# Attention and experts on one core: product with v in one step, a hand-made order, q cast on GpSimd

## The chip, the cores and the metric

One core of a Trainium2 chip runs the whole program. Its engines are TensorE (PE; PEld is its weight load), VectorE (DVE), ScalarE (ACT), GpSimd (POOL) and SyncE (SP, which issues transfers here). The metric is the time of one execution on the device in microseconds, as the median of several executions.

## The reference, cut to what matters

Attention with 8 batches, 8 heads, 576 positions and 64 values per head, then a mixture of 8 experts in which each token goes to one.

```
scores = q @ k.T / 8 + cum[i] - cum[j]        # cum = cumsum(log(clip(f)))
attn   = softmax(scores, causal)              # per batch and head, 576 x 576
x      = attn @ v                             # rows of all heads: 4608 x 512
e      = argmax(x @ w_gate); g = softmax(x @ w_gate)[e]
out    = g * (relu(x @ w1[e]) @ w2[e])        # w1: 512 x 1024, w2: 1024 x 512
```

All inputs and the output are float32.

## The kernel before, in words

**Pairs and steps.** Attention runs over 32 pairs of heads (n = 4 b + p: batch b, pair p). `attention_all` has one outer loop over n, from 0 to 33, and in it seven steps, i = 0 to 6 (lines 540 to 574). Step i of pair n issues one group of scores of pair n (`s_steps`: the causal tiles of both heads, then the last 64 queries of both heads jointly), one group of transposes of the weights of pair n - 1 (`t_steps`), and, at i = 1 and i = 4, one part of the product with v of pair n - 2 (`av`). At the other steps one task is taken off a list, `todo`, that finishes a batch (`fin_tasks`): the gate's product, rows of x divided by their sums and written to DRAM, and the routing stages of `route_stages`.

**Scores.** Scores are nearly exact in float32 though they are made of two fp32r products (`smm`, lines 263 to 273): the first has 128 rows, q's high part on rows 0 to 63 and q's low part on rows 64 to 127 (tile `qk1`), against k's high part twice; the second has 68 rows, q's high part again with four rows of sums (tile `q2`), against k's low part and four rows (tile `k2`). DVE adds the mask, writes to `sc` and keeps the smallest value (`s_red`, line 276); ACT takes the exponential and its sum (`s_exp`, line 283).

**Splitting q and k.** `split(n + 1)` at step 0 of pair n (lines 210 to 242): ACT casts q and k of `raw` to `qk1` (lines 228 and 229), a transfer on ACT's queue copies q's high part to `q2` (line 238), GpSimd subtracts for the low parts (`lo`, line 217), and SP loads the rows of sums from the DRAM tables cq and ck (lines 231 and 232). For n = 0 and 1 the rows of sums come straight from `cw` (`c_rows`, lines 244 to 255), partly on GpSimd's queue. `raw` has two buffers, and pair 2 a third; `load_pair(n + 3)` stands at step 5 of pair n, `load_v(n + 2)` at step 3.

**Transposes and product.** Transposes go to PSUM, and ACT (tiles 3 and 2) or DVE (the rest) copies them to `aT`. `av` (lines 382 to 404) has two parts: queries 320 to 575 with five blocks of keys, the last of 64 rows (`vb_t`), and queries 0 to 319 with three. Both heads' outputs share one PSUM bank, `ps_v`, and ACT copies each part to `xT`.

**Order.** The program is traced in this order, and a scheduler with a simulated timeline reorders what each engine gets, by what it takes to be ready; `tc.issue_after` holds TensorE's steps in their order. Each engine's queue then runs in order, and an instruction waits for semaphores at the head of its queue. SP's queue carries the loads and the writes of x alike.

**Hand-over to the experts.** Tokens are ranked within their expert. Expert 0's first 384 slots are filled from all batches but the last (`LATE = 1`, line 784): after batch 6's table, `early_tasks` work out the indices, gather rows from x in DRAM, and transpose them. Then `Moe.run` does the up products (`up`, line 890, 12 matmuls each) of those slots, gathers the other two blocks, and goes on with `down` (line 912). In `onehot_hi` the five products for the table (line 734) run on GpSimd, but on DVE where `last` is set, which is for b >= B - 2 (line 1103). Expert 0's w1 is split by DVE (high part, line 796) and GpSimd (low part, line 797).

Of the kernel before, what the change touches and what calls it, by code (L numbers as in the profile page):

```python
# [19 lines left out]
P = 128  # L20
# [10 lines left out]
class Ctx:  # L31
    pass

# [33 lines left out]
def setup_consts(c, tc):  # L67
    c.ident = c.const.tile([P, P], F32, name="ident")
    make_identity(tc.nc, c.ident)
    c.identr = c.const.tile([P, P], F32R, name="identr")  # L70
    tc.nc.vector.tensor_copy(c.identr, c.ident)


def attention_all(c, tc, qkT, va, vb, f, wgd, x_dram, batch_done, more_consts, extra):
# [13 lines left out]
    SO = {3: 0, 2: 512, 0: 896, 1: 1024}  # L88
    HW = 1280
    AS = 448  # L90

    with ExitStack() as st:
# [22 lines left out]
        def load_pair(n):  # L115

            pool, tag = (c.xap, "xa") if n == 2 else (c.wp, "R")
            raw = pool.tile([P, QW + 2 * S], F32, name="raw", tag=tag)
            b, p = divmod(n, NPAIR)
            for c0, c1 in ((0, QW), (QW, QW + 2 * S)) if n == 0 else ((0, QW + 2 * S),):  # L120
                for p0 in (0, HD):
                    last = nc.sync.dma_start(raw[p0 : p0 + HD, c0:c1], qkT[b, p, :, c0:c1])
            raws[n] = raw
            return last
# [6 lines left out]
        cq = dr.tile([2, NPR, 2, 640], F32, name="cq")  # L131
# [3 lines left out]
        nc.sync.dma_start(fr, f)  # L135
        load_pair(0)
        V.memset(ones, 1.0)
# [5 lines left out]
        nc.scalar.activation(warm, fr[0:1, 0:1], AF.Exp)  # L143
# [15 lines left out]
        Q2s, K2s = [], []  # L159
        for i in range(NQ):  # L160
            q2 = ap_.tile([68, QW], F32R, name=f"q2_{i}")
            k2 = ap_.tile([68, 2, S], F32R, name=f"k2_{i}")
# [4 lines left out]
            Q2s.append(q2)  # L167
            K2s.append(k2)
# [15 lines left out]
        setup_consts(c, tc)  # L184

# [4 lines left out]
        def late_consts():  # L190
            V.memset(wg, 0.0)
            for j in range(2):
                nc.sync.dma_start(
# [6 lines left out]
        vts, xTs, ssums, jsums = {}, {}, {}, {}  # L200

        def load_v(n):
            b, p = divmod(n, NPAIR)
            va_t = io.tile([P, 4, 2, HD], F32, name="va_t")
            vb_t = io.tile([64, 2, HD], F32, name="vb_t")
            nc.sync.dma_start(va_t, va[b, p])
            nc.sync.dma_start(vb_t, vb[b, p])
            vts[n] = (va_t, vb_t)

        def split(n):  # L210
            q2, k2 = Q2s[n % NQ], K2s[n % NQ]
            raw = raws.pop(n)
            qk1 = c.qp.tile([P, QW + 2 * S], F32R, name="qk1", tag="Q")
            q2c = q2[64:66].bitcast(F32).rearrange("r (j s) -> r j s", j=2)
            k2c = k2[66:68].bitcast(F32)
            k2l = k2[0:64].rearrange("p j s -> p (j s)")
            lo = lambda eng, o, p0, c0, c1: eng.tensor_tensor(  # L217
                o, raw[p0 : p0 + 64, c0:c1], qk1[p0 : p0 + 64, c0:c1].bitcast(F32),
                ALU.subtract,
            )  # L220
            if n == 0:
                nc.scalar.copy(qk1[:, 0:QW], raw[:, 0:QW])
                nc.scalar.copy(qk1[:, QW:], raw[:, QW:])  # L223
                nc.scalar.copy(q2[0:64], raw[0:64, 0:QW])
                lo(V, qk1[64:128, 0:QW], 64, 0, QW)
                lo(V, k2l, 0, QW, QW + 2 * S)
            else:
                nc.scalar.copy(qk1[:, 0:QW], raw[:, 0:QW])  # L228
                nc.scalar.copy(qk1[:, QW:], raw[:, QW:])
                if n > 1:  # L230
                    nc.sync.dma_start(q2c, cq[:, n].rearrange("j r s -> r j s"))
                    nc.sync.dma_start(
                        k2c.rearrange("r j s -> r (j s)"), ck[n].rearrange("r j s -> r (j s)")
                    )
                if n == 1:
                    V.tensor_copy(q2[0:64], raw[0:64, 0:QW])
                else:
                    nc.scalar.dma_start(q2[0:64].bitcast(F32), qk1[0:64, 0:QW].bitcast(F32))
                eng = V if n == 1 else nc.gpsimd
                lo(eng, qk1[64:128, 0:QW], 64, 0, QW)  # L240
                lo(eng, k2l, 0, QW, QW + 2 * S)
            ops[n] = (qk1, qk1[:, QW:].rearrange("p (j s) -> p j s", j=2), q2, k2)

        def c_rows(n):

            q2c = Q2s[n][64:66].bitcast(F32).rearrange("r (j s) -> r j s", j=2)
            k2c = K2s[n][66:68].bitcast(F32)

            eng = nc.sync if n == 0 else nc.gpsimd
            eng.dma_start(k2c[:, 0, :], cwf[n : n + 1, :, 0:S])  # L250
            eng.dma_start(q2c[:, 0], cwf[n : n + 1])
            hb = NPR + n
            nc.gpsimd.dma_start(k2c[:, 1, 0:512], cwf[hb : hb + 1, :, 0:512])
            nc.gpsimd.dma_start(k2c[:, 1, 512:S], cwf[hb : hb + 1, :, S:640])
            return eng.dma_start(q2c[:, 1], cwf[hb : hb + 1])
# [31 lines left out]
        def s_tiles(n, items):  # L287
# [9 lines left out]
            for j, t in items:  # L297
# [3 lines left out]
                s_exp(n, d, w, 5 * j + t,  # L301
                      ssums[b][:, t, 2 * p + j : 2 * p + j + 1])
                o += w

        def s_joint(n, half):
            b, p = divmod(n, NPAIR)
# [3 lines left out]
            s_red(n, 2 * HW + half * JW, pb[:, 0:JW], m, 10 + half,  # L310
                  1.0e38 if half == 0 else nms[n][:, 10:11])
            if half == 1:
# [858 lines left out]
```

## Time and profile before

| | us |
|---|---|
| median of 3 runs | 901.28 (899.35 to 906.79) |
| profiled execution | 898.03 |
| its span, first to last instruction | 896.3 |
| TensorE busy | 841.6 |
| DVE busy | 499.9 |
| ACT busy | 432.9 |
| GpSimd busy | 298.5 |

The execution's own time is 1.7 us over its span. A matmul counts as busy from its issue to its modelled end, and matmuls overlap, so a busy TensorE can still have gaps in it. Attention takes the time up to some 415 us, the experts the rest, some 57 us an expert.

### The profile page before, as it was taken

How to read it: one execution, taken by the hardware profiler on the slowest of the kernel's cores; microseconds unless marked ns; L12 is line 12 of the kernel's file. 1: busy time of each engine (PE TensorE's matmuls, PEld its weight loads, DVE VectorE, ACT ScalarE, POOL GpSimd, SP SyncE). 2: the span in 40 equal slices, each digit the busy share in tenths (PEclk: the TensorE clock that was granted, in tenths of full speed). 3: DMA queues.
4: the chain of work that ended last, by engine and by line, in shares of the span. 5: the costliest groups of instructions: out<-in, count | busy, mean ns of one | idle time of the engine just before them, and what ended most of it. 6: DMA issues, size and time to landing. Idle time of an engine off the chain costs nothing.

```text
span 896.3 us, 15462 instructions
## 1 busy us (share of the span) xinstructions
PE 841.6 (94%) x5664; PEld 719.8 (80%) x5664; DVE 499.9 (56%) x1487; ACT 432.9 (48%) x1069; POOL 298.5 (33%) x230
## 2 busy tenths in 40 slices
PE   3699999999999999979999999999999999999993
PEld 2576878777777878667889989889899898998982
DVE  6455867777777768686537254542545425444310
ACT  5698889888888888742121212312222122231210
POOL 6454464646464636331052031220311203102010
PEclk9899999999999999989999999999999999999997
DMA  7877887878787879324246054350441515305000
GB/s 166 206 177 166 201 188 192 192 185 197 169 202 172 196 174 237 105 87 125 82 153 208 34 175 131 104 165 36 165 135 62 177 63 165 114 25 162 11 36 17
DMA packets 42006, 124.49 MB, mean 139 GB/s; under 512 B 7427, under 2 KB 9475, under 8 KB 37960
## 3 DMA queue, kind: packets, MB, share of 16 engines
q1 hardware_dynamic: 32904, 93.68, 40.0%
q0 software_dynamic: 6624, 19.96, 6.3%
q10 hardware_dynamic: 2400, 9.83, 5.4%
q8 instruction: 46, 0.75, 0.4%
q14 instruction: 32, 0.26, 0.1%
HBM read 94.07 MB, written 20.55 MB: 128 GB/s over the span
## 4 chain that ended last, share of the span: by engine, by line
PE 80%; ACT 6%; DMA 5%; DVE 5%; issue 2%; POOL 1%; SPq 1%; ACTq 0%; DVEq 0%; POOLq 0%
PE ps L890 25%; PE ps L912 24%; PE ps L269 10%; PE ps L395 8%; DMA raw<-in_qkT 4%; PE ps L333 4%; ACT sc L283 2%; PE ps L352 2%; PE ps L452 2%; DVE sc L276 2%; PE ps L430 2%; ACT aT L324 1%; PE ps L855 1%; PE ps L363 1%; DVE aT L322 1%
## 5 line engine op out<-in xcount | busy, mean ns | idle before, releaser
L912 PE MATMUL ps<-w,hh 128*128 128x512 f32 x640 | 197.8, 392 | 0.0
L283 ACT ACTIVATE sc<-sc,nmx 128x512 f32<-128x512 f32 (+4 forms) x288 | 167.0, 585 | 15.6 <-DVE nmx L276 15.4
L276 DVE CUSTOM_DVE_ANT_0 sc<-ps,mask 128x512 f32<-128x512 f32 (+4 forms) x288 | 132.1, 483 | 70.4 <-PE ps L269 69.7
L895 ACT ACTIVATE hh<-ps 128x384 fp32r<-128x384 f32 (+1 forms) x128 | 56.1, 438 | 199.5 <-PE ps L890 199.5
L919 POOL DMA_INDIRECT out<-y,si_fast x37 | 41.5, 1121 | 313.1 <-ACT y L918 297.0
L890 PE MATMUL ps<-xa,w 128*128 128x384 f32 x768 | 144.7, 336 | 0.0
L269 PE MATMUL ps<-qk 128*128 128x288 f32 (+4 forms) x384 | 129.3, 368 | 11.9 <-DVE qk L217 11.3
L896 DVE SCALAR_TENSOR_TENSOR hl<-ps,hh 128x384 fp32r<-128x384 f32 (+1 forms) x128 | 62.6, 489 | 136.7 <-ACT hh L895 136.7
L912 PEld LDWEIGHTS ps<-w,hh 128*128 128x128 f32 x640 | 118.5, 188 | 21.8
L890 PEld LDWEIGHTS ps<-xa,w 128*128 128x128 f32 x768 | 132.8, 188 | 1.1
L217 POOL TENSOR_TENSOR k<-raw,qk 64x1152 fp32r<-64x1152 f32 x30 | 79.9, 2665 | 141.5 <-PE ps L269 71.0
L912 PE MATMUL ps<-w,hl 128*128 128x512 f32 x320 | 123.7, 392 | 0.0
L269 PE MATMUL ps<-k,q 68*128 68x288 f32 (+4 forms) x384 | 106.8, 326 | 5.3 <-DMA k<-cw 2.7
L890 PE MATMUL ps<-xb,w 128*128 128x256 f32 x768 | 103.2, 285 | 0.7 <-ACT xb L860 0.7
L890 PEld LDWEIGHTS ps<-xb,w 128*128 128x128 f32 x768 | 100.1, 192 | 3.5 <-ACT xb L860 0.8
L395 PE MATMUL ps<-aT,va_t 128*64 128x256 f32 (+3 forms) x896 | 98.8, 360 | 0.9 <-issue 0.8
L217 POOL TENSOR_TENSOR qk<-raw,qk 64x1280 fp32r<-64x1280 f32 x30 | 87.5, 2915 | 20.8 <-ACT qk L228 18.9
L918 ACT ACTIVATE y<-ps,g_fast 128x512 f32<-128x512 f32 x37 | 25.5, 690 | 135.9 <-PE ps L912 129.8
L796 DVE CAST w<-wraw 128x1024 fp32r<-128x1024 f32 x64 | 44.5, 704 | 83.0 <-PE ps L912 50.8
L269 PEld LDWEIGHTS ps<-qk 128*128 128x128 f32 x384 | 70.9, 198 | 22.1 <-ACT qk L223 11.3
L395 PEld LDWEIGHTS ps<-aT,va_t 128*64 128x64 f32 x896 | 59.5, 138 | 35.4 <-issue 9.7
L333 PE MATMUL ps<-ident,sc 128*128 128x128 f32 x512 | 80.7, 281 | 2.5 <-ACT aT L324 2.4
(159 smaller groups left out, 1095.1 us busy)
## 6 DMA issues: line engine op xcount, KB each, us to landing
raw<-in_qkT SPq DMA_DIRECT2D x62, 608.0 KB
wraw<-in_w SPq DMA_DIRECT2D x64, 512.0 KB
q<-qk ACTq DMA_DIRECT2D x30, 320.0 KB
va_t<-in_va SPq DMA_DIRECT2D x32, 256.0 KB
x_dram<-row SPq DMA_DIRECT2D x32, 256.0 KB
vb_t<-in_vb SPq DMA_DIRECT2D x32, 32.0 KB
x_dram<-row SPq DMA_DIRECT2D x8, 128.0 KB
raw<-in_qkT SPq DMA_DIRECT2D x2, 320.0 KB
```

The source lines that it names most:

```text
L217: lo = lambda eng, o, p0, c0, c1: eng.tensor_tensor(o, raw[p0 : p0 + 64, c0:c1], qk1[p0 : p0 + 64, c0:c1].bitcast(F32), ALU.subtract,)
L269: note(nc.tensor.matmul(out, ql[:, q0 : q0 + P], kl[:, j, k0 : k0 + kw], start=(i == 0), stop=(i == last),))
L276: V.tensor_tensor_reduce(scs[n][:, dst : dst + src.shape[1]], src, m, -0.125, init, ALU.add, ALU.min, nms[n][:, col : col + 1],)
L283: nc.scalar.activation(x, x, AF.Exp, bias=nms[n][:, col : col + 1], scale=-1.0, accum_out=acc)
L333: note(nc.tensor.transpose(pt[:, o : o + P], sc[:, s0 : s0 + P], c.ident))
L395: c.last_av = note(nc.tensor.matmul(pv[j * HD : (j + 1) * HD, q0 - qa : qb - qa], l, r, start=(blk == 0), stop=(blk == nb - 1),))
L796: V.tensor_copy(w[:, 0], raw)
L890: nc.tensor.matmul(ph[:, 0:n], w[:, wi, fs], x[:, xi, kt, :], start=(k == 0), stop=(k == 3 * KT - 1),)
L895: nc.scalar.activation(hh[:, ft, :], ph[:, 0:n], AF.Relu)
L896: nc.vector.scalar_tensor_tensor(hl[:, ft, :], ph[:, 0:n], 0.0, hh[:, ft, :].bitcast(F32), ALU.max, ALU.subtract,)
L912: nc.tensor.matmul(py, hi_[:, ft, ms], w[:, wi], start=(k == 0), stop=(k == 3 * FT - 1),)
L919: nc.gpsimd.indirect_dma_start(out=self.out, out_offset=bass.IndirectOffsetOnAxis(ap=si[:, s : s + 1], axis=0), in_=y, in_offset=None, bou ...
```

## The change

The product with v of pair n - 2 is one step, at i = 1, with its two parts in the banks `ps_v` and `ps_m`; its last block has 68 rows, of which v's last four are zeros. The joint scores move to the front of `sc`, so that 68 columns can be transposed there. For pairs from 2 on GpSimd makes q's high and low parts two pairs ahead (`q_parts`, step 5) and, a pair ahead at step 2, copies q's high part to `q2` and makes k's low part (`copies`); ACT makes k's high part at step 1 (`k_first`). Every third raw has the third buffer, the loads of raw move to step 2 (step 4 in pair 0), and those of v to step 3 of their own pair. Pair 1's casts come ahead of pair 0's scores, and all first rows of sums go over SP. `InOrder.pin` holds each engine but TensorE, through all pairs but the first, to the order of the program. In a step, the copies of transposes now stand ahead of the step's exponentials. Rows of x are written three steps after they are made, except in the last batch, and the transfer of jsum goes to ACT's queue. Finishing a batch starts a pair later, at the product's step, and up to one task goes with each of the other six steps (two where the list is long); the gate's two parts go together. `LATE` is 2, so that the early gather follows batch 5; only the last batch's table products stay on DVE; five of the eight first up products stand in the last pair's steps 2 to 6; w1's high parts go to ACT, its loads and splits to fixed steps of pairs 29 to 31; the early indices are worked out with PSUM operands.

```diff
+class InOrder:
...
+    def pin(self, on=True):
+        traced = self.tc.nc.cur_bb.bb.instructions
+        for i in traced[self.at :]:
+            if on and i.engine in self.last and i.engine != mybir.EngineType.PE:
+                self.tc.add_manual_dep(
+                    i, self.last[i.engine],
+                    mybir.DependencyInfo(
+                        mybir.DependencyClass.NoSync, mybir.DependencyReason.DATA
+                    ),
+                    reason="in order",
+                )
+            self.last[i.engine] = i.name
+        self.at = len(traced)
...
-    SO = {3: 0, 2: 512, 0: 896, 1: 1024}
+    SO = {3: S, 2: S + 512, 0: S + 896, 1: S + 1024}
...
+    KB = 68
...
+            if n not in raws:
+                pool, tag = (c.xap, "xa") if n % 3 == 2 else (c.wp, "R")
+                raws[n] = pool.tile([P, QW + 2 * S], F32, name="raw", tag=tag)
+            raw = raws[n]
...
+        sp_dma(fr, f)
         load_pair(0)
+        load_pair(1, (0,))
...
+        vbs = [ap_.tile([KB, 2, HD], F32, name=f"vb_{i}") for i in range(3)]
+        for vb_t in vbs:
+            nc.gpsimd.memset(vb_t[64:KB], 0.0)
...
+        def first_casts(n):
+            qk1, raw, q2 = operands(n), raws[n], Q2s[n]
+            pin = tc.keep_in_program_order
+            pin(nc.scalar.copy(qk1[:, 0:QW], raw[:, 0:QW]))
+            if n == 0:
+                pin(nc.scalar.copy(q2[0:64], raw[0:64, 0:QW]))
+            else:
+                nc.gpsimd.tensor_copy(q2[0:64], raw[0:64, 0:QW])
+            pin(nc.scalar.copy(qk1[:, QW:], raw[:, QW:]))
+        def first_seconds(n):
+            qk1, k2 = ops[n][0], ops[n][3]
+            first = lo(V, n, qk1[64:128, 0:QW], 64, 0, QW)
+            if n == 1:
+                tc.keep_in_program_order(first)
+                lo(nc.gpsimd, n, k2[0:64].rearrange("p j s -> p (j s)"), 0, QW, QW + 2 * S)
+            else:
+                for j in range(2):
+                    lo(V, n, k2[0:64, j], 0, QW + j * S, QW + (j + 1) * S)
+            raws.pop(n)
+        def q_parts(n):
+            qk1, raw = operands(n), raws[n]
+            nc.gpsimd.tensor_copy(qk1[:, 0:QW], raw[:, 0:QW])
+            lo(nc.gpsimd, n, qk1[64:128, 0:QW], 64, 0, QW)
+        def k_first(n):
+            nc.scalar.copy(ops[n][0][:, QW:], raws[n][:, QW:])
+        def copies(n):
+            _, _, q2, k2 = ops[n]
+            nc.gpsimd.tensor_copy(q2[0:64], raws[n][0:64, 0:QW])
+            lo(nc.gpsimd, n, k2[0:64].rearrange("p j s -> p (j s)"), 0, QW, QW + 2 * S)
+            raws.pop(n)
...
+        def c_rows(n, j):
+            q2c, k2c = Q2s[n][64:66].bitcast(F32), K2s[n][66:68].bitcast(F32)
+            r = cwf[j * NPR + n : j * NPR + n + 1]
+            if j == 0:
+                sp_dma(k2c[:, 0, :], r[:, :, 0:S])
+                sp_dma(q2c[:, 0:640], r)
             else:
...
+                sp_dma(k2c[:, 1, 0:512], r[:, :, 0:512])
+                sp_dma(k2c[:, 1, 512:], r[:, :, S:640])
+                sp_dma(q2c[:, 640:], r)
...
+        def e_tiles(n, items):
+            b, p = divmod(n, NPAIR)
+            for j, t in items:
+                s_exp(n, j * HW + SO[t], P * (t + 1), 5 * j + t,
                       ssums[b][:, t, 2 * p + j : 2 * p + j + 1])
...
+            note(nc.tensor.transpose(pt[0:KB, 0:P], sc[:, 512 : 512 + KB], c.ident))
...
+        def av(n):
...
+            va_t, vb_t = vts.pop(n)
+            xT, aT = xTs[b], aTs.pop(n)
+            for (qa, qb, nb), bank in zip(AV, (ps_v, ps_m)):
+                pv = psum(bank)
+                for blk in range(nb):
+                    q0 = max(qa, P * blk)
+                    for j in range(2):
+                        if blk < 4:
+                            l, r = va_t[:, blk, j, :], aT[:, j, AS * blk + q0 : AS * blk + qb]
+                        else:
+                            l, r = vb_t[:, j, :], aT[0:KB, j, 1024:1088]
+                        c.last_av = note(nc.tensor.matmul(
+                            pv[j * HD : (j + 1) * HD, q0 - qa : qb - qa], l, r,
+                            start=(blk == 0), stop=(blk == nb - 1),
+                        ))
+                pvs.append((xT[:, p, qa:qb], pv[:, 0 : qb - qa]))
+            scs.pop(n)
+        def av_out():
+            for o, x in pvs:
+                nc.scalar.copy(o, x)
+            pvs.clear()
...
+                nc.scalar.dma_start(jss[b], jsum[64:128, :])
...
+            def write():
+                nc.sync.dma_start(x_dram[r0 : r0 + qn, :], xr[:qn])
+            if b < B - 1:
+                c.later.append([3, write])
+            else:
+                write()
...
+        def fin_gate(b):
...
+        first_casts(0)
+        first_seconds(0)
+        c_rows(0, 0)
+        load_pair(1, (1,))
+        c_rows(0, 1)
+        c_rows(1, 0)
+        c_rows(1, 1)
+        load_pair(2)
...
+                for x in c.later:
+                    x[0] -= 1
+                while c.later and c.later[0][0] <= 0:
+                    c.later.pop(0)[1]()
+                if n == 0:
+                    if i == 0:
+                        first_casts(1)
+                    elif i == 2:
+                        first_seconds(1)
+                elif n + 1 < NP:
+                    if i == 0:
+                        load_c(n + 1)
+                    elif i == 2:
+                        copies(n + 1)
+                if i == 5 and n + 2 < NP:
+                    q_parts(n + 2)
+                if i == 3 and n < NP:
+                    load_v(n)
+                if i == (4 if n == 0 else 2) and n + 3 < NP:
                     c.mark = load_pair(n + 3)
-                if i == 3 and n + 2 < NP:
-                    load_v(n + 2)
-                if i == 3 and n == 0:
-                    with tc.issue_after(pe_last[0]):
...
+                if i == 5 and n == 1:
+                    late_consts()
+                s_, e_ = ss[i] if ss else (None, None)
+                if s_:
+                    step(s_)
+                if ts_:
                     step(ts_[i])
...
+                if e_:
+                    e_()
+                if i == 1 and 0 < n and n + 1 < NP:
+                    k_first(n + 1)
+                if i == 1 and 2 <= n:
+                    step(lambda: av(n - 2))
+                    av_out()
+                    fb, fp = divmod(n - 2, NPAIR)
+                    if fp == 0 and 1 <= fb < B - 1:
+                        step(lambda: fin_gate(fb - 1))
+                        todo += fin_tasks(fb - 1)
+                    elif fp == NPAIR - 1 and fb >= B - 2:
+                        todo += [lambda fb=fb: fin_gate(fb)] + fin_tasks(fb)
                 else:
-                    for k in range(2 if len(todo) > 18 else 1):
-                        fin_bank[0] = ps_v if i == 6 and k == 0 else ps_m
+                    for k in range(2 if len(todo) > 28 else 1):
+                        fin_bank[0] = ps_m if (i + k) % 2 == 0 else ps_v
                         if todo:
                             step(todo.pop(0))
-                if p == 0 and n > 0 and i in (1, 3, 6):
-                    fin_sums(b - 1, i // 3)
-                extra(n, i)
+                at = {(0, 1): 0, (1, 0): 1, (1, 1 if b == B else 4): 2}.get((p, i))
+                if n >= NPAIR and at is not None:
+                    fin_sums(b - 1, at)
+                for f in extra(n, i):
+                    step(lambda: note(f()))
+                order.pin(n > 0)
...
-        V.tensor_copy(w[:, 0], raw)
+        if eng is None:
+            V.tensor_copy(w[:, 0], raw)
+        else:
+            self.nc.scalar.copy(w[:, 0], raw)
         (eng or V).tensor_tensor(w[:, 1], raw, w[:, 0].bitcast(F32), ALU.subtract)
...
             [self.early_index] + [lambda m=m: self.fetch(0, m) for m in range(NA)]
-            + [lambda m=m: self.turn(0, m) for m in range(NA)]
+            + [lambda: None] * 6 + [lambda m=m: self.turn(0, m) for m in range(NA)]
...
-                for ft in range(FT):
+                for ft in range(self.ups, FT):
                     self.up(0, 0, ft)
...
-        return route_stages(c, tc, b, lg_of, b >= B - 2), moe.early_tasks() if b == B - 1 - LATE else []
+        return route_stages(c, tc, b, lg_of, b == B - 1), moe.early_tasks() if b == B - 1 - LATE else []
+    loads = {(last - 2, 4): 0, (last - 1, 0): 3, (last - 1, 4): 2, (last, 0): 1}
+    splits = {(last - 1, 2): 0, (last - 1, 5): 3, (last, 1): 2, (last, 4): 1}
     def extra(n, i):
-        for kt, at in enumerate(((last - 1, 4), (last - 1, 6), (last, 3), (last + 1, 0))):
-            if (n, i) == at:
-                with tc.issue_after(c.mark.ins):
-                    moe.load_w1(0, kt)
+        if (n, i) in splits:
+            moe.split_w1(0, splits[n, i])
+        if (n, i) in loads:
+            moe.load_w1(0, loads[n, i])
+        if n != last + 1 or i < 2:
+            return []
+        if i == 2:
+            moe.begin_h(0, 0)
+        return [lambda: moe.up(0, 0, i - 2)]
```

## Rows read from the trace of the kernel before

**Rows 1.** The page's totals: busy us, share of the span, instructions.
```profile
PE 841.6 (94%) x5664; PEld 719.8 (80%) x5664; DVE 499.9 (56%) x1487; ACT 432.9 (48%) x1069; POOL 298.5 (33%) x230
```

**Rows 2.** Windows: start:end, length, busy us of PE, PEld, DVE, ACT, POOL, PEclk, DMA, GB/s.
```profile
36.00:60.00 24.00, 20.22 (x145) 16.75 (x146) 11.89 (x43) 21.48 (x53) 14.05 (x5) 0.86 0.75 164
...
60.00:382.00 322.00, 314.39 (x2561) 247.64 (x2560) 236.07 (x964) 272.98 (x735) 171.22 (x105) 1.00 0.78 184
...
382.00:403.00 21.00, 16.13 (x118) 12.90 (x119) 17.07 (x55) 9.93 (x28) 7.36 (x4) 0.81 0.27 82
```

**Rows 3.** Chain of waits, gate of the batches: start us, us, what.
```profile
132.34 1.73 PE ps L452 x8
...
366.11 1.75 PE ps L452 x8
```

**Rows 4.** Timeline, product of one pair: start us, us, what, [idle before].
```profile
294.77 1.06 PEld L395 LDWEIGHTS ps<-aT,va_t 128*64 128x64 f32 x12 [0.17 <-issue]
...
295.90 0.53 PE L269 MATMUL ps<-qk 128*128 128x288 f32 x2
...
300.39 1.49 PEld L395 LDWEIGHTS ps<-aT,va_t 128*64 128x64 f32 x16 [0.17 <-ACT qk L228]
...
302.16 0.19 PEld L395 LDWEIGHTS ps<-aT,vb_t 64*64 64x64 f32 x4 [0.28 <-issue]
...
302.43 0.44 PE L269 MATMUL ps<-qk 128*128 128x384 f32 x1
...
302.53 0.19 PEld L269 LDWEIGHTS ps<-k,q 68*128 68x128 f32 x1
```

**Rows 5.** Lines: engine, operation, tiles, count | busy us, mean ns | idle before, releaser.
```profile
L217 POOL TENSOR_TENSOR qk<-raw,qk 64x1280 fp32r<-64x1280 f32 x30 | 87.5, 2915 | 20.8 <-ACT qk L228 18.9
...
L217 POOL TENSOR_TENSOR k<-raw,qk 64x1152 fp32r<-64x1152 f32 x30 | 79.9, 2665 | 141.5 <-PE ps L269 71.0 <-ACT gT L457 49.5 <-DMA raw<-in_qkT 20.8
...
L228 ACT CAST qk<-raw 128x1280 fp32r<-128x1280 f32 x31 | 39.2, 1263 | 36.4 <-DMA raw<-in_qkT 21.9 <-PE ps L269 11.4 <-PE ps L363 1.9
...
L734 POOL TENSOR_TENSOR Rr<-eqh,vals 128x240 bf16<-128x240 bf16 x30 | 16.6, 581 | 0.0
...
L163 POOL MEMSET q<- 4x1280 f32 x2 | 2.4, 1198 | 0.3 <-POOLq L1159 0.3
```

**Rows 6.** Waits: who waited for whom: us in total, times, longest.
```profile
PE ps L352 <- DVE aT L322: 10.3, 11, 5.4
...
PE ps L373 <- DVE aT L322: 5.5, 2, 4.1
```

**Rows 7.** Timeline, the start.
```profile
16.98 0.79 PE L269 MATMUL ps<-k,q 68*128 68x512 f32 x1 [2.67 <-DMA k<-cw]
...
27.30 1.18 SPq L122 DMA_DIRECT2D raw<-in_qkT  x2
...
36.31 1.26 ACT L228 CAST qk<-raw 128x1280 fp32r<-128x1280 f32 x1 [3.56 <-DMA raw<-in_qkT]
...
38.71 1.11 PE L352 MATMUL ps<-ident,sc 128*128 128x128 f32 x4 [5.37 <-DVE aT L322]
...
41.79 1.05 PE L363 MATMUL ps<-ident,sc 128*128 128x128 f32 x4
```

**Rows 8.** Timeline, the end of attention.
```profile
391.71 3.83 DVE L734 TENSOR_TENSOR Rr<-eqh,vals 128x240 bf16<-128x240 bf16 x5
...
397.08 0.42 PE L373 MATMUL ps<-ident,sc 128*64 128x128 f32 x1 [4.13 <-DVE aT L322]
...
401.95 3.40 PE L395 MATMUL ps<-aT,va_t 128*64 128x256 f32 x16
```

**Rows 9.** Timeline, the last batch's routing and first gathered rows.
```profile
431.52 0.21 DVE L674 CAST ohb<-pr 128x48 bf16<-128x48 f32 x1
...
440.05 0.20 PE L690 MATMUL pr<-ohb,trib 128*128 128x48 bf16 x1
...
454.34 0.53 PE L855 MATMUL ps<-identr,xg 128*128 128x128 f32 x4 [0.75 <-DMA xg<-x_dram,gi_fast]
```

More of the change, by code (lines that the diff above doesn't have):

```diff
@@ L158, in attention_all, with const_rows @@
         NQ = 2
[L159 to L162, printed above, removed]
+        Q2s = [ap_.tile([68, QW], F32R, name=f"q2_{i}") for i in range(NQ)]
+        K2s = [ap_.tile([68, 2, S], F32R, name=f"k2_{i}") for i in range(NQ)]
+        def const_rows(i):
+            q2, k2 = Q2s[i], K2s[i]
             nc.gpsimd.memset(q2[64:68].bitcast(F32), -8.0)
@@ L204, in load_v @@
             va_t = io.tile([P, 4, 2, HD], F32, name="va_t")
[L205 to L207 removed]
+            vb_t = vbs[n % 3]
+            sp_dma(va_t, va[b, p])
+            sp_dma(vb_t[0:64], vb[b, p])
             vts[n] = (va_t, vb_t)
[L210 to L242 removed]
@@ L496, in fin_tasks @@
                 fx[1], expert, fx[2], gate, rank, fx[3], slot, fx[4], hi, lo,
-                idle, table,
+                idle, idle, table,
             ]
@@ L590, in setup_routing @@
     nc = tc.nc
+    V = nc.vector
     rp = c.rp
     nt = B * 5
+    c.identr = c.const.tile([P, P], F32R, name="identr")
+    V.tensor_copy(c.identr, c.ident)
     c.iota128 = rp.tile([P, P], F32, name="iota128")
@@ L777, in table_indices, with table_indices_psum @@
     return gi, si, g
+def table_indices_psum(c, pool, tab, n):
+    V = c.nc.vector
+    ps = lambda i: c.ps_r[:, 168 + 3 * i : 168 + 3 * i + n]
+    t = pool.tile([P, n], F32, name="ti_early")
+    gi = pool.tile([P, n], U32, name="gi_early")
+    si = pool.tile([P, n], U32, name="si_early")
+    g = pool.tile([P, n], F32, name="g_early")
+    V.tensor_scalar(ps(0), tab[:, 1, :], 64.0, None, ALU.mult)
+    V.tensor_tensor(gi, ps(0), tab[:, 0, :], ALU.add)
+    V.tensor_tensor(t, ps(0), tab[:, 0, :], ALU.add)
+    V.tensor_scalar(ps(1), tab[:, 2, :], -BIG, BIG, ALU.mult, ALU.add)
+    V.tensor_tensor(si, ps(1), t, ALU.add)
+    V.tensor_scalar(ps(2), tab[:, 3, :], 1.0, None, ALU.mult)
+    V.tensor_tensor(ps(2), ps(2), tab[:, 4, :], ALU.add)
+    V.tensor_tensor(g, ps(2), tab[:, 5, :], ALU.add)
+    return gi, si, g
 NA, NB = 3, 2
 CA, CB = NA * P, NB * P
-LATE = 1
+LATE = 2
 class Moe:
@@ L889, in up @@
             for wi, xi in ((0, 0), (1, 0), (0, 1)):
[L890 removed]
+                mm = nc.tensor.matmul(
                     ph[:, 0:n], w[:, wi, fs], x[:, xi, kt, :],
```

201 lines of the change are left out of this document (81 added, 120 removed).

## The prediction, made before the change was run

> **What bounds the kernel now.** I read the page's totals first: TensorE is busy for 841.6 of 896.3 us, ACT for 432.9 and GpSimd for 298.5 [rows 1]. Then the stretches. The change touches only attention and the hand-over to the experts, up to some 470 us. Ahead of 36 us TensorE mostly waits. From 60 to 382 us, 322 us of attention, it is busy for 314.4 us at the full 2.4 GHz, ACT for 273.0, DVE for 236.1, GpSimd for 171.2 [rows 2]: TensorE is the bound, and ACT at 85% is next. So a gain has three possible places: the 7.6 idle us in that stretch, gaps inside "busy" TensorE, and the two ends of attention. There the mean granted clock was 0.86 (36 to 60 us) and 0.81 (382 to 403 us) [rows 2], so some of that time was at 1.2 GHz, each time behind a long idle piece.
>
> The length of a pair comes from the gate's matmuls, once per batch: 132.34 and 366.11 us are five batches apart [rows 3], so 46.75 us a batch and **11.69 us a pair**.
>
> **1. Product with v in one step, and 68 rows instead of 64.** In the trace one pair's product is two visits. The first loads 16 weights from 300.39 us; its last block, 64 rows by 64 columns, is loaded after a gap of 0.28 us, and the scores go on at 302.43: 2.04 us. The second lasts from 294.77 to 295.90: 1.13 us, with a gap of 0.17 us ahead of its first load [rows 4]. Without the 0.17 the second visit is 0.96 us for 576 streamed columns (320+192+64), and the first, up to the 64-row block, 302.16-300.39-0.17 = 1.60 us for 960: both 1.667 ns a column. So the work is (960+64+576) x 1.667 = 2.67 us, and the rest of the 3.17 us, 0.50 us, is changes of tile form. The new step enters once (0.17) and has no 64-row tile: its last block has 68 rows, as the scores' second operand has, whose load overlaps the matmul of the 128-row one without a gap (302.53) [rows 4]. That is 2.84 us. It saves 0.33 us a pair, x32 = **-10.5 us**, all on TensorE's own path. Bounds: 0 (the gaps stay, or another engine sets the pace) and -16 (0.50 x 32). The gate's two parts also become one visit, each in its own bank; at 0.17 for a form change, 8 x 0.17 = -1.5, between 0 and -2.3 (0.28 each).
>
> **2. q off ACT, and an SBUF copy off the DMA.** Per pair ACT loses a 1.26 us cast, and its queue a 64x1280 transfer; GpSimd gains a 128x1280 cast and a 64x1280 copy. That cast stood in ACT's queue and waited for raw 21.9 us in all [rows 5]; exponentials and copies stood behind it, then DVE's copies, then TensorE's transposes, which waited for DVE 10.3 us in 11 cases, one of them 5.4, and 5.5 in two others, one of them 4.1 [rows 6]. In the new order GpSimd waits for raw, nine steps ahead of need. The two long waits belong to steps 3 and 4. Of the rest, 4.9+1.4, and other crumbs of the 7.6, I take half: **-4**, between +4 and -7.6.
>
> GpSimd's price is the unknown. No one-input copy of this size is in the trace. Nearest rows: filling 1280 columns, 1.20 us, and the two-input subtraction on 1280 columns, 2.92 us [rows 5]. A copy reads one operand where a fill reads none and a subtraction two: I take the middle, 2.0 us each. GpSimd then has per pair 2.92+2.67+2x2.0 = 9.6, and per batch five products of 0.58 [rows 5] and some 0.7 for the sums, 0.9 a pair: 10.5 us, under the 11.2 or so that TensorE keeps. At 1.2 it is 8.9; at 2.9 it is 12.3 and GpSimd is the bound (rival B).
>
> The Trainium skill, "GPSIMD Engine Reference", Engine selection, says that a one-input operation runs there at roughly line rate, against half of VectorE's speed for two inputs. By it a copy is about 1.1 us, an estimate; the sum stays as it is and rival B falls away; no run here shows it yet.
>
> **3. The start.** TensorE's second matmul group waits 2.67 us for k's sum rows, which GpSimd's queue sent behind its setup [rows 7]. Later it waits 5.37 us in one piece, to 38.71: ACT stood at the cast for pair 3, whose raw came at 36.31 [rows 7]. SP issued that load at 27.30 only, behind the v loads and the tables [rows 7], though pair 0's buffer had long been free. The change puts it at step 4 of pair 0, the sum rows on SP right behind the first loads, and v last. Against that, ACT now does pair 1's two casts, 2.4 us, ahead of pair 0's exponentials. Raw of pair 1 should be there near 14 us, so these start near 16.5; at 273.0/322 x 11.69 = 9.9 us of ACT a pair, less 2.4 of casts, they end near 24, and pair 1's steps, at ACT's 9.9-1.26 = 8.6, near 32.6. Before, they ended with the transposes at 41.79+1.05, still 1.05 us for four [rows 7]. That is -10; for late constants, now in pair 1, I take 1 off: **-9**, between -3 (only the 2.67 goes) and -13 (both waits, 8.0, and 5 for matmuls at half clock).
>
> **4. The end of attention.** At 391.71 DVE takes five products for batch 6's table, 3.83 us; the last pair's reductions stand behind them, TensorE waits 4.13 us to 397.08, and its matmuls then run at half speed, the product's 16 in 3.40 us from 401.95 [rows 8] against 1.77 [rows 4]. The change gives DVE only the last batch's products (b == B-1); batch 6's go to GpSimd, 5 x 0.58 us with a table matmul due five steps on. Saved: 4.13, and half of some 7.5 us of slow matmuls up to 405.3. **-7.5**, between -3 (another wait takes its place) and -8.
>
> **5. Early gather a batch earlier, five up products inside the last steps.** TensorE gets these ups behind the last pair's product, as before: work that is moved, with nothing idle under it that a row shows but 0.75 us for the first gathered rows at 454.34 [rows 9]. In the new list the last batch's gate stands behind batch 6's remaining tasks and three of the ups. I take **0**; rival C prices it. W1's high parts go from DVE to ACT and its low parts stay on GpSimd, all under pairs 30 and 31.
>
> **6. Fixed order on DVE, ACT, GpSimd and SP.** An instruction that waits now holds all behind it. ACT's two copies of the product stand ahead of the next step's copy and exponential; in front of them are this step's copy, exponential and k cast, together about the 2.84 us that the product lasts. SP's v loads, which waited for the product's buffers with sum rows and raw behind them, come two pairs later and find a free buffer; x's rows are written when they are long done, so SP stands at neither. SP's raw loads still wait for GpSimd; behind them stand v and sum rows, due five steps on or later. The jsum transfer moves to ACT's queue, once a batch. For new waits I put **+4**, 0.13 us a pair, between 0 and +12 (0.4 a pair, the 4.9 us of rows 6 over its 10 small cases being 0.5 each).
>
> **Sum.** -10.5-1.5-4-9-7.5+0+4 = -28.5 against this execution's 898.03 us (span 896.3 and 1.7 around it): 869.5. The execution lies 3.25 us under the median of the runs, 901.28; I put 2.5 of that back: **872 us**.
>
> **Rivals.**
> A. ACT and DVE in fixed order, not TensorE, set the pair's length. For: ACT is at 85%, and its waits now count in full. Against: it loses 1.26 of 9.9 us. Then steps 1 and 2 bring nothing (+16) but the ends stay: 888.
> B. The other side: GpSimd becomes the bound, in q_parts and copies. It decides from copies of about 2.4 us each (11.2-6.5, halved). At the subtraction's 2.92 us, with 0.3 us of waiting ahead of each of its two blocks, a pair is 2.92+2.67+5.84+0.9+0.6 = 12.9 us against 11.69; 30 pairs make +36, the ends -16.5: 918. For: its subtraction costs 2.3 ns a column. Against: the fill's 0.94.
> C. The last batch's routing comes too late: its gate waits for three ups of 12 matmuls of 384 columns, 6 us at 2.4 GHz, and the gathered rows come as much later, with a stretch at half clock behind the idle: +8, 880. Against: ohb was ready at 431.52 and its matmul came at 440.05 [rows 9], 8 us of slack.
> D. The change doesn't do what it says: with 68 rows the gap stays, and half of step 1's gain goes: 877.
>
> **Chances.** As forecast 0.60, A 0.16, C 0.09, D 0.07, B 0.08. Low end: start -13, small waits -7.6, no new waits: 872-4-3.6-4 = 860; with the last end's -0.5 and step 1's rest, 857. High end 894, past A and short of B. About 1% (9 us) is what a measurement of this kernel can tell from none. Faster by more than that, under 892: forecast, C, D and over half of A: 0.85. Within: 0.09, from A and B. Slower: 0.06, most of B.
>
> **What would show it.** Right: one visit of about 2.8 us to the product in a pair, no gap ahead of its last block; batches some 44 us apart; neither the 5.37 nor the 4.13 us wait, and less time at half clock; GpSimd's copies at or under 2 us. Wrong: copies near 2.9 us and TensorE waiting for GpSimd in each pair; ACT without idle time; pair 1's last transposes no earlier than 42 us; a wait of over 5 us for the last batch's gathered rows.

## The result, and the profile after the change

The changed kernel takes **908.77 us** in the median (906.35 to 910.44) against 900.88 for the kernel before, a ratio of 1.0085 (95% interval 1.0065 to 1.0104): a little slower, where 872 us had been forecast. The profiled execution takes 909.53 us, 11.5 more than the one before.

The page's totals and its chain, by engine, and below them the chain of the kernel before:

```profile
PE 833.4 (92%) x5664; PEld 717.9 (79%) x5664; DVE 491.6 (54%) x1478; ACT 407.8 (45%) x1043; POOL 377.5 (42%) x293
...
PE 70%; DVE 13%; ACT 7%; DMA 4%; issue 2%; POOL 2%; SPq 0%; ACTq 0%; POOLq 0%; DVEq 0%
```
```profile
PE 80%; ACT 6%; DMA 5%; DVE 5%; issue 2%; POOL 1%; SPq 1%; ACTq 0%; DVEq 0%; POOLq 0%
```

TensorE works 8.2 us less than in [rows 1] in a span 11.5 us longer, and DVE, busy for 54% of the span, holds 13% of the chain, where it held 5%. By stretches (windows, columns as in [rows 2]):

```profile
36.00:60.00 24.00, 17.51 (x140) 14.40 (x141) 12.69 (x51) 14.65 (x38) 14.32 (x13) 0.81 0.69 144
60.00:382.00 322.00, 298.71 (x2509) 242.12 (x2507) 226.25 (x942) 245.75 (x698) 239.62 (x163) 0.99 0.64 153
382.00:403.00 21.00, 18.16 (x131) 13.93 (x131) 11.49 (x43) 14.50 (x39) 8.16 (x4) 0.84 0.27 80
```

From 60 to 382 us TensorE has lost 15.7 busy us against [rows 2], though no engine is near full: ACT has 76%, GpSimd 74%, DVE 70%. The gate's matmuls, once per batch, in the chain:

```profile
136.16 1.11 PE ps L523 x16
...
329.29 1.11 PE ps L523 x16
```

Four batches in 193.13 us are 48.3 a batch, against 46.75 before. Yet the product itself came out as forecast. One pair's, from the timeline:

```profile
98.65 1.49 PEld L458 LDWEIGHTS ps<-aT,va_t 128*64 128x64 f32 x16 [0.17 <-issue]
100.16 0.31 PEld L458 LDWEIGHTS ps<-aT,vb 68*64 68x64 f32 x4
100.38 1.06 PEld L458 LDWEIGHTS ps<-aT,va_t 128*64 128x64 f32 x12
101.51 0.19 PEld L328 LDWEIGHTS ps<-qk 128*128 128x128 f32 x1
```

One visit of 2.86 us, one gap of 0.17 at its entry, none ahead of the 68-row block [rows 4]. GpSimd's lines:

```profile
L245 POOL TENSOR_TENSOR qk<-raw,qk 64x1280 fp32r<-64x1280 f32 x30 | 87.6, 2920 | 4.0 <-DMA xg<-x_dram,gi_early 1.7
...
L283 POOL CAST qk<-raw 128x1280 fp32r<-128x1280 f32 x30 | 37.5, 1250 | 4.1 <-DMA raw<-in_qkT 4.1
L292 POOL CAST q<-raw 64x1280 fp32r<-64x1280 f32 x30 | 37.4, 1246 | 1.6 <-PE ps L328 0.2
```

The copies take 1.25 us, near the fill of [rows 5]. So neither rival B nor D happened. What did happen stands in the waits, TensorE's in the whole span and ACT's from 60 to 382 us, the last line being that of the kernel before:

```profile
PE ps L393 <- DVE aT L382: 15.3, 14, 7.9
PE ps L423 <- DVE aT L382: 12.9, 18, 1.4
...
PE ps L434 <- DVE aT L382: 5.4, 11, 0.7
...
ACT sc L342 <- DVE nmx L335: 58.8, 63, 2.6
```
```profile
ACT sc L283 <- DVE nmx L276: 2.8, 3, 1.4
```

TensorE now waits for DVE's copies in small pieces all through attention: without the longest, of 7.9 us, these three lines make 25.7 us, and the two of [rows 6] without their longest 6.3. ACT waits 58.8 us for DVE's reductions, where it waited 2.8. The timeline of DVE and TensorE shows how, inside one step with a task:

```profile
103.02 0.28 PE L328 MATMUL ps<-k,q 68*128 68x128 f32 x1
...
103.87 0.29 DVE L382 COPY aT<-ps 128x128 f32<-128x128 f32 x1 [0.74 <-ACT aT L384]
104.08 0.19 DVE L782 TENSOR_REDUCE pr<-ex 128x5 f32<-128x40 f32 x1
104.30 0.17 DVE L783 TENSOR_SCALAR pr<-pr 128x5 f32<-128x5 f32 x1
...
105.58 0.17 DVE L786 CAST vals<-pr 128x5 bf16<-128x5 f32 x1
105.66 0.55 DVE L335 CUSTOM_DVE_ANT_0 sc<-ps,mask 128x384 f32<-128x384 f32 x1
...
106.68 0.30 PE L434 MATMUL ps<-ident,sc 128*68 128x128 f32 x1 [0.59 <-DVE aT L382]
...
108.88 0.63 PE L423 MATMUL ps<-ident,sc 128*128 128x128 f32 x4 [1.36 <-DVE aT L382]
```

The scores were ready at 103.30. Their reduction begins at 105.66, behind a copy that waits for ACT and the gate task's eight tiny operations; by the list of tasks, the products that read their values come five tasks later. The start has a wait of the same sort, longer than any before:

```profile
30.55 2.62 POOL L245 TENSOR_TENSOR k<-raw,qk 64x1152 fp32r<-64x1152 f32 x1
31.07 2.18 DVE L696 CAST identr<-ident 128x128 fp32r<-128x128 f32 x1
...
38.48 0.19 POOL L707 IOTA iota<- 128x40 f32 x1
38.71 0.18 DVE L710 TENSOR_SCALAR iota5m<-iota 128x40 f32<-128x40 f32 x1 [5.45 <-POOL iota L707]
39.69 1.24 POOL L292 CAST q<-raw 64x1280 fp32r<-64x1280 f32 x1
39.72 1.31 DVE L726 CAST vals<-iotap 128x40 bf16<-128x40 f32 x1
...
42.05 1.12 PE L393 MATMUL ps<-ident,sc 128*128 128x128 f32 x4 [7.88 <-DVE aT L382]
```

DVE, tied to the late constants, stands 5.45 us until GpSimd, tied to its q parts, makes an iota (a row of index numbers); pair 1's last reductions and copies stand behind it, TensorE waits 7.88 us, and its four transposes then take 1.12 us, as in [rows 7].

### The profile page after: what moved, and what is told of

Read it like the earlier page. It is cut to its first block, busy times and chain, and to the rows that moved or that the text cites. A ratio compares the mean times of both kernels' runs of the same rounds, so it can differ in the third digit from the quotient of the medians.

```text
span 907.8 us, 15286 instructions
## 1 busy us (share of the span) xinstructions
PE 833.4 (92%) x5664; PEld 717.9 (79%) x5664; DVE 491.6 (54%) x1478; ACT 407.8 (45%) x1043; POOL 377.5 (42%) x293
## 4 chain that ended last, share of the span: by engine, by line
PE 70%; DVE 13%; ACT 7%; DMA 4%; issue 2%; POOL 2%; SPq 0%; ACTq 0%; POOLq 0%; DVEq 0%
PE ps L1028 24%; PE ps L1051 24%; PE ps L458 7%; PE ps L328 5%; DVE sc L335 4%; PE ps L393 4%; DVE aT L382 3%; ACT sc L342 3%; ACT aT L384 2%; PE ps L423 2%; DMA x_dram<-row 2%; DVE row L499 1%; PE ps L993 1%; PE ps L523 1%; DMA raw<-in_qkT 1%
## 5 line engine op out<-in xcount | busy, mean ns | idle before, releaser
L335 DVE CUSTOM_DVE_ANT_0 sc<-ps,mask 128x512 f32<-128x512 f32 (+4 forms) x288 | 129.5, 479 | 94.4 <-PE ps L328 92.5
L328 PE MATMUL ps<-qk 128*128 128x288 f32 (+4 forms) x384 | 128.6, 366 | 10.8 <-ACT qk L265 10.7
L245 POOL TENSOR_TENSOR k<-raw,qk 64x1152 fp32r<-64x1152 f32 x31 | 83.4, 2690 | 68.2 <-ACT qk L287 51.3
L393 PE MATMUL ps<-ident,sc 128*128 128x128 f32 x512 | 83.4, 287 | 15.7 <-DVE aT L382 15.3
L458 PE MATMUL ps<-aT,va_t 128*64 128x256 f32 (+3 forms) x896 | 94.3, 353 | 0.0
L393 PEld LDWEIGHTS ps<-ident,sc 128*128 128x128 f32 x512 | 59.0, 145 | 33.2 <-DVE aT L382 27.7
L922 DVE CAST w<-wraw 128x1024 fp32r<-128x1024 f32 x60 | 41.4, 699 | 79.9 <-PE ps L1051 54.8
L382 DVE COPY aT<-ps 128x128 f32<-128x128 f32 (+2 forms) x160 | 71.4, 446 | 20.5 <-ACT aT L384 20.5
```

The source lines that it names most:

```text
L245: return eng.tensor_tensor(o, raws[n][p0 : p0 + 64, c0:c1], ops[n][0][p0 : p0 + 64, c0:c1].bitcast(F32), ALU.subtract,)
L328: note(nc.tensor.matmul(out, ql[:, q0 : q0 + P], kl[:, j, k0 : k0 + kw], start=(i == 0), stop=(i == last),))
L335: V.tensor_tensor_reduce(scs[n][:, dst : dst + src.shape[1]], src, m, -0.125, init, ALU.add, ALU.min, nms[n][:, col : col + 1],)
L382: V.tensor_copy(dst, src)
L393: note(nc.tensor.transpose(pt[:, o : o + P], sc[:, s0 : s0 + P], c.ident))
L458: c.last_av = note(nc.tensor.matmul(pv[j * HD : (j + 1) * HD, q0 - qa : qb - qa], l, r, start=(blk == 0), stop=(blk == nb - 1),))
```

## The experiments

An engine is called tied where `InOrder.pin` holds it to program order, and free where the planner, the scheduler with the simulated timeline, places its instructions.

**Theory 1**: DVE's fixed order, which puts tasks and constants ahead of reductions and copies, ate the gains. **Rivals**: another engine's order; the new list of tasks. All ratios are to the kernel before, with 95% intervals; its medians ran from 899.0 to 900.9 us beside the different runs, so differences of medians between runs are good to some 2 us.

**free_all**: no engine tied.
```diff
-                order.pin(n > 0)
+                order.pin(False)
```


> The changed kernel without its fixed order: no engine is tied to program order in attention, the planner places DVE's, ACT's, GpSimd's and SP's instructions as in the kernel before. All other parts of the change stay. Theory 1 (the fixed order ate the gain of the single product step: DVE meets the routing's small operations ahead of the next step's reductions and copies, and the constants ahead of pair 1's): batches go from 48 to about 45.5 us, and the wait of 7.9 us at the start shrinks: 909 becomes 880 to 888. Theory 2 (the new list of tasks and the later writes cost it, whatever the order): 905 to 912.

888.14 us, 0.988 (0.9848 to 0.9912): the order it is, not the list.

**free_dve**: all tied but DVE.
```diff
-            if on and i.engine in self.last and i.engine != mybir.EngineType.PE:
+            if on and i.engine in self.last and i.engine not in (
+                mybir.EngineType.PE, mybir.EngineType.DVE
+            ):
```


> The changed kernel with DVE alone taken out of the fixed order; ACT, GpSimd and SP stay tied. Theory 1 (DVE's order is the cause): within 4 us of the kernel with no engine tied, 880 to 890. Rival (ACT's, GpSimd's or SP's order is the cause, DVE only shows the wait): 903 to 912, while the kernel with no engine tied is faster. If DVE and another both matter, it lies halfway.

**877.39 us**, 0.9757 (0.9739 to 0.9776): 31.4 us less than the changed kernel, and 10.8 less than with no engine tied. So tying ACT, GpSimd and SP gains, and DVE's tie alone costs more than the whole change brings. Its windows, ACT's wait and two of its gates:

```profile
60.00:382.00 322.00, 308.83 (x2667) 255.03 (x2665) 238.33 (x990) 257.19 (x734) 246.27 (x165) 1.00 0.65 161
382.00:403.00 21.00, 21.00 (x152) 17.41 (x151) 12.38 (x30) 4.16 (x10) 3.38 (x9) 1.00 0.20 54
...
ACT sc L344 <- DVE nmx L337: 21.0, 29, 1.9
...
129.20 1.11 PE ps L525 x16
...
309.87 1.11 PE ps L525 x16
```

The gates, four batches apart, make 45.2 a batch. The gate task of the same batch in DVE's timeline: the planner lets reductions pass between its operations.

```profile
97.42 0.17 DVE L788 CAST vals<-pr 128x5 bf16<-128x5 f32 x1
97.72 0.56 DVE L337 CUSTOM_DVE_ANT_0 sc<-ps,mask 128x384 f32<-128x384 f32 x1
98.20 0.09 DVE L337 DVE_READ_ACCUMULATOR2_ANT nmx<- 128x1 f32 x1
98.20 0.17 DVE L790 TENSOR_TENSOR pr<-pr,vals 128x5 f32<-128x5 f32 x1
98.27 0.28 DVE L337 CUSTOM_DVE_ANT_0 sc<-ps,mask 128x128 f32<-128x128 f32 x1
```

**dve_only**: DVE alone tied (`i.engine == mybir.EngineType.DVE`).

> The changed kernel with DVE alone in fixed order; ACT, GpSimd and SP are placed by the planner. Theory 1 (DVE's order costs it by itself): batches near 48 us, 900 to 915, against 888 with no engine tied. Rival (the cost comes from DVE's and ACT's fixed orders meeting, each waiting for the other): 885 to 893.

919.06 us, 1.0223 (1.0206 to 1.024): more than theory 1 said, and 30.9 more than with no engine tied. DVE's tie needs no other to cost, and costs the same without them.

**before_tied**: the kernel before, with DVE alone tied.
```diff
+            if on and i.engine in self.last and i.engine == mybir.EngineType.DVE:
...
+                order.pin(n > 0)
```


> The kernel before with one edit: DVE's instructions in attention tied to program order. If tying DVE is dear by itself, whatever the product, the casts or the list of tasks are: 915 to 930 against 900. Rival (it is dear only with the changed list of tasks and TensorE's shorter step): 897 to 905.

921.44 us, 1.0229 (1.0192 to 1.0266): one edit on the old kernel costs 20.9 us, so it does not take the new list of tasks. The waits are others there: from 60 to 382 us DVE stands 14.4 us for TensorE's matmuls for the table, and these stand 11.8 us for GpSimd's products.

**consts_early**: the late constants traced at step 3 of pair 0.
```diff
-                if i == 5 and n == 1:
-                    late_consts()
+                if i == 3 and n == 0:
+                    with tc.issue_after(pe_last[0]):
+                        late_consts()
```


> The changed kernel with the block of late constants (gate weights, routing's iotas and fills) traced where it stood before, at step 3 of pair 0, which isn't tied. All else stays. Theory 1 (DVE stood 5.5 us at the constants for GpSimd's iota, and TensorE's wait of 7.9 us to 42 us with the half clock behind it follows from that): the wait goes, 8 to 12 us less: 897 to 901. Rival (pair 1 is late for another reason, its casts on ACT or its sum rows): the wait stays, 906 to 911.

901.94 us, 1.0015 (1.0002 to 1.0028): 6.8 us less than the changed kernel. Pair 0 isn't tied, so the constants come both earlier and untied. The start's block was real, and a fifth of DVE's price.

**free_tasks**: of DVE's instructions, the tasks' alone untied.
```diff
+            if i.name in self.tasks:
+                continue
...
+                            order.task(lambda: step(todo.pop(0)))
```


> The changed kernel; of the fixed order only DVE's instructions of the finishing tasks (logits, routing, x's rows, table) are freed. Reductions, copies and the late constants on DVE stay tied, ACT, GpSimd and SP too. Theory 1 (these small operations, tied ahead of the next step's reductions and copies, set the pace of the steps with a task): batches at about 45.3 us in place of 48, the start's wait of 7.9 us stays: 883 to 890. Rival (the order of the reductions and copies among themselves costs it): batches stay at 47.5 to 48.5 us, 903 to 912.

889.24 us, 0.9892 (0.9876 to 0.9909): 19.5 of the 31.4 us.

**free_tasks_consts**: both edits, those of free_tasks and consts_early.

> The changed kernel with two of DVE's three tied parts undone: the tasks' instructions free, the late constants traced at step 3 of pair 0; reductions and copies stay tied. If the parts add up (19.5 us for the tasks, 7 for the constants): 880 to 884, and what is left to 877 is the reductions and copies tied among themselves. If they overlap: 886 to 890.

884.82 us, 0.9817 (0.9791 to 0.9842): another 4.4 by the medians, which lies between the two expectations, or 6.7 by the ratios. What is left to free_dve, 7.4 by the medians or 5.4 by the ratios, is put down to reductions and copies tied among themselves, which was not tried alone.

**late_tasks**: tied, but the tasks' DVE instructions behind the next step's reductions and copies.
```diff
+        new = traced[self.at :]
+        held, self.held = self.held, [i for i in new if i.name in self.tasks]
+        for i in [i for i in new if i.name not in self.tasks] + held:
```


> The changed kernel with every engine still tied, but on DVE a task's instructions are tied behind the reductions and copies of the step after, in place of ahead of them. Nothing else moves. Theory 1 as a matter of place (a reduction must not stand behind a task's chain): batches at 45.5 to 46.5 us, 886 to 898 with the start's wait left. Rival (any fixed place costs as much, since DVE must wait for each task's inputs wherever it stands): 903 to 912.

920.44 us, 1.0233 (1.0216 to 1.025): worse, against theory 1 as I had put it. Another wait has come up in place of the old ones:

```profile
PE ps L503 <- DVE row L507: 14.7, 10, 2.4
```

The transposes of x's rows now wait for a bank that DVE empties a step later; in the changed kernel this wait came to 2.7 us.

**split_tasks**: tied, expert and gate each cut into two tasks.
```diff
-                fx[1], expert, fx[2], gate, rank, fx[3], slot, fx[4], hi, lo,
+                fx[1], expert, expert2, fx[2], gate, gate2, rank, fx[3], slot, fx[4], hi, lo,
```


> The changed kernel, all engines tied, with the two tasks that give DVE the longest chains (expert, six instructions, and gate, eight) each cut into two tasks in steps of their own. The same work in smaller lumps. If the lump in one step is what TensorE's two or three banks cannot cover: 1 us a batch less, 899 to 904. Rival (a fixed place ahead of the reductions costs the same in lumps of any size): 906 to 912.

929.21 us, 1.0339 (1.0287 to 1.0391). The cut moved the table's addition to just ahead of a product, and the planner put its matmuls into the product:

```profile
124.78 0.28 PE L859 MATMUL pr<-Rr,Ar 128*128 128x240 bf16 x1
...
126.44 0.28 PE L859 MATMUL pr<-Rr,Ar 128*128 128x240 bf16 x1
...
126.76 0.41 DVE L863 TENSOR_TENSOR tab<-tab,pr 128x240 f32<-128x240 f32 x1 [3.46 <-PE pr L859]
127.08 0.68 DVE L335 CUSTOM_DVE_ANT_0 sc<-ps,mask 128x512 f32<-128x512 f32 x1
```

DVE stands 3.46 us for an addition that no engine is waiting for, with a reduction behind it. So this time tells nothing of lumps.

**split_tasks2**: the same cut, the table at its old step.
```diff
-                fx[1], expert, fx[2], gate, rank, fx[3], slot, fx[4], hi, lo,
-                idle, idle, table,
+                fx[1], expert, expert2, fx[2], gate, gate2, rank, slot, hi, lo,
+                fx[3], fx[4], table,
```


> As split_tasks, all engines tied and the tasks expert and gate cut in two, but the table's task keeps its old step: the last two writings of x's rows move behind it in place of the two empty tasks. In split_tasks the table's addition fell just ahead of the product's step, the planner put its matmuls into the product, and DVE, tied, waited 3.5 us for them with the reductions behind it, 23 us in 60 to 382 us; so its time didn't tell of lumps. If the lump in one step is what costs: 898 to 904. If lumps of any size cost the same in a fixed place: 906 to 914.

910.54 us, 1.0099 (1.007 to 1.0128): no gain. Cutting these two lumps brings nothing; two writings of x's rows moved with them, which was not tried alone.

**one_product** and **one_product4**: the product's step alone, in the kernel before.
```diff
-            vb_t = io.tile([64, 2, HD], F32, name="vb_t")
+            vb_t = vbs[n % 4]
...
-                if i in (1, 4) and 2 <= n:
-                    step(lambda: av(n - 2, i // 4))
...
+                if i == 1 and 2 <= n:
+                    step(lambda: av(n - 2))
...
```
This is one_product4; one_product has three tiles (`n % 3`).

> The kernel before with only the product changed: one step in place of two, its last block with 68 rows in place of 64 (four zero rows in v), joint scores laid out first. Casts, order, tasks and start stay as before. The price of step 1 of the prediction, 0.33 us a pair: 10.5 us less than the kernel before, ratio 0.986 to 0.991. If another engine had set the pair's length already: ratio 0.997 to 1.003.

933.93 us, 1.0387 (1.0368 to 1.0407), which tells nothing of the product: with three tiles v's rows were overwritten while in use, the routing came out another, and the loop for experts that overflow ran.

> The kernel before with only the product changed, as in one_product, but with four tiles for v's last rows in place of three, because v is loaded two pairs ahead there and with three tiles a load overwrote rows still in use (one_product then computed another routing, and its time says nothing of the product). Step 1 of the prediction, 0.33 us a pair: ratio to before 0.986 to 0.991. If another engine sets the pair's length already: 0.997 to 1.003.

888.23 us, 0.9871 (0.9855 to 0.9888): 10.8 us, against 10.5 forecast. In its trace the gates at 92.56 and 319.93 us, five batches apart, make 45.5 a batch against 46.75, or 0.32 us a pair against the 0.33 worked out. The total agrees in part by chance: in that trace the wait of 5.37 us of [rows 7] has become 8.48.

**free_dve_q_act**: DVE free, q's cast back on ACT.
```diff
-            nc.gpsimd.tensor_copy(qk1[:, 0:QW], raw[:, 0:QW])
+            nc.scalar.copy(qk1[:, 0:QW], raw[:, 0:QW])
```


> The kernel with DVE free, but q's 128x1280 cast goes back from GpSimd to ACT (at the place where GpSimd had it; the 64x1280 copy stays on GpSimd). Step 2 of the prediction undone: ACT, tied, gets 30 x 1.26 us more, 92% of the stretch from 60 to 382 us, and holds exponentials behind raw: 881 to 890 against 877. Rival (ACT has room, the cast's place is of no account): 876 to 879.

885.67 us, 0.9839 (0.981 to 0.9869): 8.3 us over free_dve, in a kernel whose ACT is tied.

**free_dve_consts**: DVE free and the constants early.

> The two edits that helped, together: DVE out of the fixed order and the late constants traced at step 3 of pair 0. With DVE free, TensorE still waited 4.0 us to 44.98 us, with half clock behind it: two constant casts on DVE took 3.32 and 1.28 us and ended when a GpSimd instruction ended. If that block goes: 869 to 874 against 877. Rival (the iotas then delay the first pairs' operands on GpSimd and the wait only moves): 876 to 880.

877.25 us, 0.975 (0.972 to 0.978): nothing, though TensorE is busy all 24 us from 36 to 60 (20.0 without it). Attention's last gate came 2.3 us earlier; the wait for the first gathered rows, 4.3 us in both, came all the same. Of the 2.3 us, 1.3 went behind it: in the chain the next 36 matmuls of the up products take 6.68 us at a mean granted clock of 0.61 (434 to 441 us), against 5.41 at 0.78 (436 to 442 us) in free_dve. Where the rest went is not settled.

**free_dve_products**: DVE free, batch 6's five table products back on DVE (`b >= B - 2`).

> The kernel with DVE free, but the five table products of the last batch but one go back to DVE, as in the kernel before (step 4 of the prediction undone). As predicted, 4.1 us of waiting and slow matmuls come back near the last pairs: 881 to 885 against 877. Rival (in the new list they lie beside other work): 876 to 879.

878.63 us, 0.9762 (0.973 to 0.9795): no difference.

**free_dve_ups0** and **free_dve_products_ups0**: the five up products back behind attention (`self.ups = 0`), the second with batch 6's products on DVE too.

> The kernel with DVE free, but the five up products of the first expert that stand in the last pair's steps go back behind attention (step 5 of the prediction undone). Theory: they are what keeps TensorE busy between the last pairs' steps (21.0 of 21.0 us from 382 to 403, against 16.1 before), and step 5, priced at nothing, brought what step 4 was to bring: 882 to 887 against 877. Rival (moved work, as predicted): 876 to 879.

**874.71 us**, 0.9726 (0.9686 to 0.9767), the lowest median of the study, though its interval overlaps that of free_dve: the up products were no cover.

> As the kernel with DVE free and the last batch but one's five table products on DVE, and the five up products back behind attention too (steps 4 and 5 of the prediction undone together). If the up products were the cover of DVE's five: 4 us or more over the same kernel with the products on GpSimd. Rival (DVE's five cost nothing because they take 1.67 us here and not 3.83, with GpSimd idle beside them): within 1.5 us of it.

875.66 us, 0.9738 (0.9697 to 0.9779): the five cost nothing even then. The timeline of free_dve_products shows them, and that of the kernel before what stood beside [rows 8]:

```profile
386.91 1.67 DVE L839 TENSOR_TENSOR Rr<-eqh,vals 128x240 bf16<-128x240 bf16 x5
```
```profile
391.88 2.44 POOL L797 TENSOR_TENSOR w<-wraw,w 128x1024 fp32r<-128x1024 f32 x1 [6.08 <-DVE w L796]
```

## Why the prediction was wrong

**Step 6 failed**: "For new waits I put +4, 0.13 us a pair, between 0 and +12". DVE's tie costs 31.4 us by itself, the ties of ACT, GpSimd and SP gain 10.8, together +20.6. The parts of DVE's: 19.5 for the tasks, 7 for the constants (4.4 by the medians once the tasks are free), the rest for reductions and copies. I had bounded it by ten small waits of TensorE [rows 6], which are what the planner's order left over; what the tie undoes is that order itself, and no row of waits shows it. I walked through ACT's and SP's queues in the new order, not through DVE's, where most small operations stand.

**Step 1** was right: 0.32 us a pair for 0.33, by the mechanism named. The gate's share in it was not tried alone, and its 8 x 0.17 makes 1.4, not 1.5. **Step 2** was right in sign and too small: 8.3 against 4, beyond its own bound of 7.6, though measured with ACT tied. GpSimd's copies take 1.25 us, where I took 2.0. The Trainium skill's line rate for one input ("GPSIMD Engine Reference", Engine selection), which I had weighed, agrees with the trace.

**Step 3** came out up to its last term: pair 1's steps ended on TensorE at 31.66 us, where I had worked out 32.6 and [rows 7] give 42.84, though the wait of 2.67 us for sum rows did not go (2.28, now for q's). The last term failed: I took 1 us off for late constants in pair 1, and they cost 6.8; pair 2's steps ended at 53.29 us, 1.0 before those of the old kernel. **Step 4**: the wait of 4.13 us did go, but not for the reason given. On DVE the five products take 1.67 us with GpSimd idle beside them and 3.83 with one of its subtractions, and undoing the edit costs under 1.5 us. **Step 5**, priced at nothing: its up products cost nothing that can be told (2.7 us by the medians); the earlier gather was not tried alone.

**Rival A** named the mechanism for DVE, but let it eat the gains of steps 1 and 2 only (888); tying DVE on the old kernel shows that it costs by itself. B and D are out. C came in part: waits of 1.97, 0.86 and 0.79 us for gathered rows against 0.75 [rows 9].

With DVE free the time, 877.39 us, lies inside the range given for the changed kernel, but that is luck. With no engine tied, steps 1 to 5 together bring 12.2 us (888.14 against 900.30) where 32.5 had been forecast, little more than step 1 alone; the other 10.8 come from the ties of ACT, GpSimd and SP, where the sum had a loss. The working of the low end is off too: step 1's rest is 5.5, which with the 0.5 makes 854, not 857.

**Open**: why a fixed place costs 19.5 us for the tasks. Cutting two lumps and one later place were tried and are no remedies; how much is the tasks' own length ahead of the reductions, and how much what they wait for, was not separated. Which of the three other ties gains the 10.8 was not tried.

## What to carry to other kernels

A fixed order is priced on each engine by walking its queue: what would stand behind an instruction whose input is late, and who needs that next. On this kernel it paid to tie the engines whose work comes in the order in which it is needed, and to leave free the one that mixes deadlines, DVE with reductions due at once and routing due steps later. Busy shares (70% here) don't show it; on a tuned kernel a tie can be tried alone first, on the old code.

## What the hardware showed unasked

Some DVE operations that read and write SBUF take longer while GpSimd works there, and no wait is listed for them. In the changed kernel the cast to `identr` took 2.18 us, to 33.25, when GpSimd's subtraction from 30.55 ended at 33.17; the cast to `vals` took 1.31, to 41.03, when a GpSimd copy ended at 40.93. In the kernel with DVE free the cast to `identr` stands at 10.59 us and takes 0.34, but there the cast to `trib` took 3.32, to 43.10, when a GpSimd subtraction ended at 43.01, and TensorE waited 4.00 us, to 44.98. The five products are another case, 3.83 against 1.67.

The Trainium skill ("SBUF — State Buffer", SBUF: two separate sides) has the two engines share a port pair that one of them locks for a whole instruction, DVE when its operation is in a two-port mode or has two SBUF inputs. The ends of the casts agree with it, though no run tested it alone; the five products are merged in the view, so which of them stood isn't shown. It bore on [rows 8], and I had not applied it.
